# A fused attention, expert and MLP kernel: the order of the down products, the place of the small matmuls, and which engine takes the residuals

## The chip, the cores and the metric

The kernel runs on one core of a Trainium2 chip. The metric is the device time of one execution in microseconds (us), the median of three runs.

## The reference

Three layers follow each other, all in float32. Attention works in chunks of 64 positions; its result x (2304 tokens of 512) goes through a dense mixture of 8 experts, whose weights P come from eight rounds of Sinkhorn normalisation, and then through an MLP with a maximum of three products.

```python
attn = softmax(q_c @ k_c.T / 8)            # 4 x 8 heads, chunks of 64, head_dim 64
x = (attn @ v_c) -> (2304, 512)
logits = x @ w_gate; P = exp(logits - logits.max())
for _ in range(8):
    P /= P.sum(1, keepdims=True) + 1e-09
    P /= P.sum(0, keepdims=True) + 1e-09
    P *= N / E
out = sum over e of P[:, e:e+1] * (relu(x @ w1[e]) @ w2[e])     # F = 1024
h = max(out @ w1, out @ w2, out @ w3)                           # 768 wide
return h @ w_out
```

## The kernel before, in words

**Precision.** Every large product is made of three matmuls of a rounded type: high part by high part, high by low, low by high. So each operand exists twice: a copy in the rounded type (xh, wh, hh) and the residual that is left (xl, wl, hl). The helper `hilo` makes both: ScalarE copies, then GpSimd (or VectorE, where an engine is passed) subtracts.

**Items.** The 2304 tokens are split into three thirds of 768. The work is a list of items: 32 for each third of the expert layer (256 hidden units each, four to an expert), items 0 to 95, and then 9 for each third of the second MLP, items 96 to 122. In `up(n)` an item makes its hidden block by a seven-product scheme on 2 x 2 blocks: products P0 to P6, each of six matmuls with 384 columns, into three PSUM tiles: pa (P0, P2, P4, P6), pg (P1, P5) and pb (P3). The tiles keep accumulating, so between two products into one tile an evacuation must be done: ScalarE copies P0, P1 and P2 out as s0, s1 and s2 (L242), VectorE adds them to pb, pa and pg after P3, P4 and P5, as c0, c1 and c2 (L245). So P2 waits for s0, P4 for s2, P6 for c1, and the next item's P1 for c2. After P4 and P5 and P6, `finish` makes hh (ScalarE) and hl from c or from PSUM. In the expert items the 768-wide hl after P4 is GpSimd's (L216), after a relu in place by ScalarE (L215); the two of 384 are VectorE's (L219). In the MLP items the maximum with the earlier block is VectorE's (L227), and the last item of three (i = 2) calls `hilo` for hh and hl.

**Down products.** The hidden block of item n is used while item n + 1 runs. `down(n, q, j)` is one group: six matmuls of 512 columns into one PSUM bank, then an evacuation that adds it to the token block's accumulator, mostly on VectorE (L292, L288, L301). There are six groups an item (D1 to D6 below): first three that need hh and hl of the blocks 2 and 1, then three that need 0 and 3. The banks come from a pool of two (dn) up to item 24, and alternate between that and the other small pool (wk, two) from item 25 on. An expert item makes one group after each of P0 to P5. Of the MLP's items each of three makes two, after P2 and P4.

**What is put between.** `bg` is a table that says which functions are called at a position (item, product). At each position the order of issue is: the product and its evacuation; a transposed accumulator to be sent on (`y_out`), if one is due; preparation or fetch of weights; the functions of the table in the order in which they were entered; then the down groups. Engines run what they are given in that order. In the table stand: attention for token blocks 6 to 17 in items 1 to 13 (scores `att_qk` and `att_exp`, `att_norm` and `att_T`, `att_swap` with four DMAs, values `att_pv`, `x_save`, `gate`); the Sinkhorn steps in items 14 to 19, where `row_norm` (VectorE) is followed at the next spot by the TensorE sum `col_sum`; the decode of the second MLP's weights from 64-bit floats in items 33 to 94 (`decode_all`: 9 calls a job, in the last of which the DMA that stores dhi is issued and the next job's first VectorE step writes the same buffer); the next third's x (`x_put`, `x_cols`).

**DMAs** are all issued by SyncE, in order: raw weights, stores of the prepared weights in the first third, and from then on two fetches an item (`fetch` at P1, two items ahead, and `fetch2` at P2).

Of the kernel before, what the change touches and what calls it, by code (L numbers as in the profile page):

```python
# [47 lines left out]
def kernel(ctx: ExitStack, tc: tile.TileContext, qk, vv, wg, wts, wts2, out):  # L48
# [137 lines left out]
    mt = [None]  # L186

    def up(n):
# [21 lines left out]
        def finish(q, src):  # L210

            if not m2:
                nc.scalar.activation(out=hh[:, q], in_=src, func=AF.Relu)  # L213
                if q.start == 0:
                    nc.scalar.activation(out=src, in_=src, func=AF.Relu)  # L215
                    nc.gpsimd.tensor_tensor(out=hl[:, q], in0=src, in1=hh[:, q].bitcast(F32),  # L216
                                            op=ALU.subtract)
                    return
                nc.vector.scalar_tensor_tensor(out=hl[:, q], in0=src, scalar=0.0,  # L219
                                               in1=hh[:, q].bitcast(F32), op0=ALU.max, op1=ALU.subtract)  # L220
                return
            m = mt[0]
            if it["i"] == 0:
                if q.start == 3:
                    nc.scalar.copy(out=m[:, q], in_=src)
                return
            nc.vector.tensor_tensor(out=m[:, q], in0=src, in1=m[:, q], op=ALU.max)  # L227
            if it["i"] == 2:
                hilo(hh[:, q], hl[:, q], m[:, q])

        s = {}
        for pos, (wi, xi, b) in enumerate(PRODUCTS):
            ps = bank[b]
            for k in range(2):
                ws = slice(k * P, (k + 1) * P)
                for i, (x, y) in enumerate(((wh[n], vh), (wh[n], vl), (wl[n], vh))):
                    nc.tensor.matmul(ps, lhsT=x[:, wi, ws], rhs=y[:, xi, k], start=b not in begun,  # L237
                                     stop=k == 1 and i == 2, skip_group_check=True)
                    begun.add(b)
# [10 lines left out]
            else:  # L250
                finish(slice(3, 4), ps.unsqueeze(1))
            yield pos
# [94 lines left out]
    def x_put(pos):  # L347
        i = PRODUCTS[pos][1]
        hilo(xh[:, i], xl[:, i], xst[i], nc.vector if pos % 2 == 0 else None)
# [3 lines left out]
    def x_cols(j, r, eng, pl, xh, xl):  # L353
# [10 lines left out]
        nc.gpsimd.tensor_tensor(out=xl[:, 0:2, :, cols], in0=raw, in1=xh[:, 0:2, :, cols].bitcast(F32),  # L364
                                op=ALU.subtract)
        nc.gpsimd.tensor_tensor(out=xl[:, 2, :, cols], in0=r[:, 1, 2:4], in1=xh[:, 2, :, cols].bitcast(F32),
# [64 lines left out]
    def decode_all():  # L431
# [11 lines left out]
        for at_ in range(-2, len(jobs)):  # L443
# [13 lines left out]
            if i is not None:  # L457
                strassen_w([V[:, x] for x in range(4)], [V[:, 4 + x] for x in range(4)], nc.vector)
                yield
                hilo(hi, lo, V[:, 1:8])  # L460
                dst = lambda h: scr[p * 3 + i, h, :, :, k, :]
            else:
                hi, lo = (x[:, 0:4].rearrange("p i f -> p (i f)") for x in (hi, lo))
                hilo(hi, lo, V[:, 0:4].rearrange("p i f -> p (i f)"))
# [121 lines left out]
    def gate(t):  # L586
        p = wk.tile([P, E], F32, name="gp", tag="wk")
# [42 lines left out]
    for m in range(NT - NPE):  # L630
        t, n = NPE + m, 1 + m
        at(n, 0, lambda t=t: (att_qk(t), load_qk(t + 3), att_exp(t)))
        at(n, 2, lambda t=t: (att_norm(t), att_T(t)))
        at(n, 6, lambda t=t: att_swap(t))
        at(n + 1, 3, lambda t=t: (att_pv(t, wk), load_v(t + 3)))
        at(n + 1, 5, lambda t=t: x_save(t))
        at(n + 1, 6, lambda t=t: gate(t))
    for t in range(NPE):
        at(t // 2, 3 + 2 * (t % 2), lambda t=t: gate(t))
# [22 lines left out]
    for a in range(NPAIR + 1, first_of[3] - 1):  # L662
        for b in range(a % 2, 7, 2):
            at(a, b, lambda: next(dec, None))
# [4 lines left out]
    for k in range(1, 4):  # L669
# [6 lines left out]
        for pos in range(7):  # L676
            at(n0 - 1, pos, lambda pos=pos: x_put(pos))
# [12 lines left out]
    with tc.manual_schedule():  # L690
# [47 lines left out]
        for n in range(ni):  # L738
# [3 lines left out]
            quota = few = -(-len(pend) // ahead)  # L742
            for pos in up(n):
# [16 lines left out]
                if quota and pend and pos < 6 and (few > 2 or pos in (2, 4)):  # L760
                    down(*pend.pop(0))
                    quota -= 1
            if it["down"]:
                assert not pend
                pend = [(n, q, j) for q in (1, 0) for j in range(TS // 2)]
# [40 lines left out]
```

## Time and profile before

| | us |
|---|---|
| median of three runs | 1914.39 (1913.91 to 1915.68) |
| the profiled execution | 1914.13 |
| its span | 1912.3 |
| TensorE busy | 1869.4 (98%) |
| VectorE busy | 1126.6 (59%) |
| ScalarE busy | 689.2 (36%) |
| GpSimd busy | 638.2 (33%) |

The span is the time from the first to the last instruction of the profiled execution; the execution's own time has 1.8 us around it. Busy time of TensorE counts pipelined matmuls whose modelled ends overlap the next start, so the time between two starts says more than a duration. The profile names engines PE (TensorE), PEld (its weight loads), DVE (VectorE), ACT (ScalarE), POOL (GpSimd) and SP (SyncE); L269 is line 269 of the kernel.

### The profile page before, as it was taken

To read this page: it belongs to the slowest core of one execution; us is meant where nothing else is said; L and a number is where in the kernel's file an instruction comes from. 1 tells how busy PE (TensorE), PEld (TensorE's weight loads), DVE (VectorE), ACT (ScalarE), POOL (GpSimd) and SP (SyncE) were. 2 spreads that over 40 slices of the span, in tenths; PEclk is the share of its full clock that TensorE was granted. 3 is DMA by queue.
4 is the path that set the end of the run, shared out by engine and by line. 5 is a ranking of instruction groups with operands and counts; after the bars stand their busy time and mean duration, and the time that the engine had idled before them with its cause. 6 is when DMAs were issued, how large, how long until landed. Compare 5 with 4: busy or idle time off the path is not lost.

```text
span 1912.3 us, 26868 instructions
## 1 busy us (share of the span) xinstructions
PE 1869.4 (98%) x10397; PEld 1671.6 (87%) x10403; DVE 1126.6 (59%) x1768; ACT 689.2 (36%) x1204; POOL 638.2 (33%) x444
## 2 busy tenths in 40 slices
PE   6999999999999999999999999999999999999998
PEld 4988888888998888898889889888889888999997
DVE  7566564646784566565656655665566656545434
ACT  4554544454444232322322342222323233423221
POOL 5766666678882111111111122111211112212101
PEclk8999999999999999999999999999999999999999
DMA  7578867678888655556556665755656564757562
GB/s 249 195 280 290 305 255 274 263 281 299 320 326 312 229 202 222 212 212 234 203 212 236 220 236 190 265 203 211 215 203 249 201 237 165 268 217 277 208 252 95
DMA packets 167872, 455.30 MB, mean 238 GB/s; under 512 B 14272, under 2 KB 74688, under 8 KB 167744
## 3 DMA queue, kind: packets, MB, share of 16 engines
q1 hardware_dynamic: 167744, 453.58, 64.9%
q8 instruction: 82, 1.34, 0.3%
q14 instruction: 46, 0.38, 0.1%
HBM read 319.57 MB, written 132.38 MB: 236 GB/s over the span
## 4 chain that ended last, share of the span: by engine, by line
PE 89%; DMA 3%; DVE 3%; ACT 2%; POOL 1%; issue 1%; SPq 0%; ACTq 0%; DVEq 0%; POOLq 0%
PE dn L269 42%; PE pa L237 25%; PE pg L237 12%; PE pb L237 6%; DMA scr<-dhi 2%; PE gp L590 1%; PE s L499 1%; PE xp L578 1%; DMA w2l<-w2s 1%; PE warm L688 1%; DVE c L245 0%; DMA w2s<-w2l 0%; DVE acc L292 0%; ACT hh L213 0%; POOL wl L183 0%
## 5 line engine op out<-in xcount | busy, mean ns | idle before, releaser
L269 PE MATMUL dn<-w2h,hl 128*128 128x512 f32 x1260 | 501.1, 398 | 4.7 <-DVE hl L219 4.4
L269 PE MATMUL dn<-w2h,hh 128*128 128x512 f32 x1260 | 496.0, 394 | 5.7 <-ACT hh L213 3.5
L269 PE MATMUL dn<-w2l,hh 128*128 128x512 f32 x1260 | 498.0, 395 | 0.5 <-DMA w2l<-w2s 0.5
L292 DVE SCALAR_TENSOR_TENSOR acc<-dn,Pt,acc 128x512 f32<-128x512 f32 x438 | 327.3, 748 | 258.1 <-PE dn L269 255.2
L216 POOL TENSOR_TENSOR hl<-c,hh 128x768 fp32r<-128x768 f32 x96 | 177.9, 1854 | 842.6 <-ACT c L215 837.7
L237 PE MATMUL pa<-xh,wh 128*128 128x384 f32 x912 | 308.0, 338 | 7.1 <-ACT s L242 4.9
L237 PE MATMUL pa<-xl,wh 128*128 128x384 f32 x912 | 307.0, 337 | 0.0
L237 PE MATMUL pa<-xh,wl 128*128 128x384 f32 x912 | 305.5, 335 | 0.0
L213 ACT ACTIVATE hh<-c 128x768 fp32r<-128x768 f32 x192 | 131.7, 686 | 477.3 <-DVE c L245 476.8
L269 PEld LDWEIGHTS dn<-w2h,hl 128*128 128x128 f32 x1260 | 236.3, 188 | 58.5 <-DVE hl L219 7.8
L269 PEld LDWEIGHTS dn<-w2h,hh 128*128 128x128 f32 x1260 | 237.0, 188 | 38.7 <-ACT hh L213 5.3
L269 PEld LDWEIGHTS dn<-w2l,hh 128*128 128x128 f32 x1260 | 236.5, 188 | 30.5 <-DMA w2l<-w2s 1.2
L242 ACT COPY s<-pa 128x384 f32<-128x384 f32 x246 | 118.1, 480 | 256.7 <-PE pa L237 256.6
L237 PEld LDWEIGHTS pa<-xh,wh 128*128 128x128 f32 x912 | 171.5, 188 | 22.8 <-ACT s L242 6.8
L237 PEld LDWEIGHTS pa<-xl,wh 128*128 128x128 f32 x912 | 171.4, 188 | 13.3
L237 PEld LDWEIGHTS pa<-xh,wl 128*128 128x128 f32 x912 | 171.3, 188 | 0.0
L237 PE MATMUL pg<-xl,wh 128*128 128x384 f32 x456 | 153.8, 337 | 0.0
L237 PE MATMUL pg<-xh,wh 128*128 128x384 f32 x456 | 152.8, 335 | 0.4 <-DVE c L245 0.4
L237 PE MATMUL pg<-xh,wl 128*128 128x384 f32 x456 | 152.9, 335 | 0.0
L219 DVE SCALAR_TENSOR_TENSOR hl<-c,hh 128x384 fp32r<-128x384 f32 x96 | 111.6, 1162 | 61.7 <-ACT hh L213 61.1
L245 DVE TENSOR_TENSOR c<-pb,s 128x384 f32<-128x384 f32 x114 | 63.2, 554 | 92.3 <-PE pb L237 86.2
L242 ACT COPY s<-pg 128x384 f32<-128x384 f32 x123 | 59.1, 481 | 146.1 <-PE pg L237 145.8
(147 smaller groups left out, 2530.9 us busy)
## 6 DMA issues: line engine op xcount, KB each, us to landing
wh<-w1s SPq DMA_DIRECT2D x64, 896.0 KB, 4.6
wl<-w1s SPq DMA_DIRECT2D x64, 896.0 KB, 6.4
w2h<-w2s SPq DMA_DIRECT2D x64, 512.0 KB, 7.5
w2l<-w2s SPq DMA_DIRECT2D x64, 512.0 KB, 8.8
w1s<-wh SPq DMA_DIRECT2D x32, 896.0 KB, 7.4
w1s<-wl SPq DMA_DIRECT2D x32, 896.0 KB, 9.2
wh<-scr SPq DMA_DIRECT2D x27, 896.0 KB, 4.6
wl<-scr SPq DMA_DIRECT2D x27, 896.0 KB, 6.4
```

Source lines behind the costliest of these rows:

```text
L213: nc.scalar.activation(out=hh[:, q], in_=src, func=AF.Relu)
L216: nc.gpsimd.tensor_tensor(out=hl[:, q], in0=src, in1=hh[:, q].bitcast(F32), op=ALU.subtract)
L219: nc.vector.scalar_tensor_tensor(out=hl[:, q], in0=src, scalar=0.0, in1=hh[:, q].bitcast(F32), op0=ALU.max, op1=ALU.subtract)
L237: nc.tensor.matmul(ps, lhsT=x[:, wi, ws], rhs=y[:, xi, k], start=b not in begun, stop=k == 1 and i == 2, skip_group_check=True)
L242: nc.scalar.copy(out=s[pos], in_=ps)
L245: nc.vector.tensor_tensor(out=c[:, q], in0=ps, in1=s[other], op=ALU.add)
L269: nc.tensor.matmul(p, lhsT=h[:, hi, ts], rhs=w[:, f, :], start=(f == 0 and i == 0), stop=(f == 1 and i == 2))
L292: nc.vector.scalar_tensor_tensor(out=acc[t], in0=p, scalar=Pt[:, t, e:e + 1], in1=acc[t], op0=ALU.mult, op1=ALU.add)
L499: nc.tensor.matmul(ss[g][cs, hp, :], lhsT=a[r, hp, 0, cs], rhs=a[r, hp, 1, cs], start=True, stop=True)
L578: nc.tensor.matmul(p[64 * g:64 * g + 64, hp, :].rearrange("p (a q) -> p a q", a=2), lhsT=v[r, h * D:(h + 1) * D], rhs=aT[r, :, he, :], sta ...
L590: nc.tensor.matmul(p, lhsT=x[:, k, :], rhs=wgr[:, k, :], start=k == 0, stop=k == KD - 1)
L688: nc.tensor.matmul(p, lhsT=wones[:, 0:P], rhs=wones, start=True, stop=True)
```

## The change

Seven edits, all of order and place; the mathematics is the same.

- Down groups: expert items up to 24 make two each after P1, P3 and P5; from item 25 on three each after P2 and P5. The last item of all makes none while it runs: two groups of the item three before it are left and are run behind it, ahead of its own six.
- In the second and third third of the expert layer, the 768-wide hl is made like the others, by VectorE from c, without the relu in place.
- In the MLP's items hl is VectorE's, and issued one product later than hh (the list `later`).
- The residuals of the decode and of `x_cols` in the MLP move from GpSimd to VectorE; `x_put` swaps which of its seven residuals are VectorE's (three instead of four) and comes one position later.
- Attention in items 0 to 13: scores at position 6 of the item before (they were at 0), normalisation at 1 (2), swap at 4 (6), values at 6 of the same item (3 of the next) and in the pool dn (wk), `x_save` at 1 (5).
- Gates take PSUM from other pools; those of blocks 0 to 5 are called three at a time at position 6 of items 0 and 1 (one at a time, in items 0 to 2).
- The decode is not called in items 63 and 64.

```diff
@@ up(n), finish
-                if q.start == 0:
+                if q.start == 0 and it["sb"] == 0:
                     nc.scalar.activation(out=src, in_=src, func=AF.Relu)
                     nc.gpsimd.tensor_tensor(out=hl[:, q], in0=src, in1=hh[:, q].bitcast(F32),
                                             op=ALU.subtract)
...
             if it["i"] == 2:
-                hilo(hh[:, q], hl[:, q], m[:, q])
+                nc.scalar.copy(out=hh[:, q], in_=m[:, q])
+                later.append(lambda: nc.vector.tensor_tensor(
+                    out=hl[:, q], in0=m[:, q], in1=hh[:, q].bitcast(F32), op=ALU.subtract))
...
+            rest = later[:]
+            later.clear()
...
+            for f in rest:
+                f()
             yield pos
@@ x_put
-        hilo(xh[:, i], xl[:, i], xst[i], nc.vector if pos % 2 == 0 else None)
+        hilo(xh[:, i], xl[:, i], xst[i], nc.vector if pos % 2 else None)
@@ x_cols
+        rest = nc.gpsimd if pl is ap_ else nc.vector
-        nc.gpsimd.tensor_tensor(out=xl[:, 0:2, :, cols], in0=raw, in1=xh[:, 0:2, :, cols].bitcast(F32),
+        rest.tensor_tensor(out=xl[:, 0:2, :, cols], in0=raw, in1=xh[:, 0:2, :, cols].bitcast(F32),
...
@@ decode_all
-                hilo(hi, lo, V[:, 1:8])
+                hilo(hi, lo, V[:, 1:8], nc.vector)
...
@@ the table
-        at(n, 0, lambda t=t: (att_qk(t), load_qk(t + 3), att_exp(t)))
-        at(n, 2, lambda t=t: (att_norm(t), att_T(t)))
-        at(n, 6, lambda t=t: att_swap(t))
-        at(n + 1, 3, lambda t=t: (att_pv(t, wk), load_v(t + 3)))
-        at(n + 1, 5, lambda t=t: x_save(t))
-        at(n + 1, 6, lambda t=t: gate(t))
+        at(n - 1, 6, lambda t=t: (att_qk(t), load_qk(t + 3), att_exp(t)))
+        at(n, 1, lambda t=t: (att_norm(t), att_T(t)))
+        at(n, 4, lambda t=t: att_swap(t))
+    for m in range(NT - NPE):
+        t, n = NPE + m, 1 + m
+        at(n, 6, lambda t=t: (att_pv(t, dn), load_v(t + 3)))
+        at(n + 1, 1, lambda t=t: x_save(t))
+        at(n + 1, 6, lambda t=t: gate(t, ps_b))
     for t in range(NPE):
-        at(t // 2, 3 + 2 * (t % 2), lambda t=t: gate(t))
+        at(t // 3, 6, lambda t=t: gate(t, ps_b if t % 3 == 0 else ps_g if t % 3 == 1 else dn))
...
-            at(a, b, lambda: next(dec, None))
+            if a not in (first_of[2] - 1, first_of[2]):
+                at(a, b, lambda: next(dec, None))
...
-            at(n0 - 1, pos, lambda pos=pos: x_put(pos))
+            a = 7 * (n0 - 1) + min(pos + 1, 6 if k == 3 else 7)
+            at(a // 7, a % 7, lambda pos=pos: x_put(pos))
@@ the main loop
-            quota = few = -(-len(pend) // ahead)
+            few = -(-len(pend) // ahead)
+            quota = few if n < ni - 1 else 0
...
-                if quota and pend and pos < 6 and (few > 2 or pos in (2, 4)):
-                    down(*pend.pop(0))
-                    quota -= 1
+                if few > 2:
+                    run = (2 if pos in (1, 3, 5) else 0) if n <= NT + 6 else 3 if pos in (2, 5) else 0
+                else:
+                    run = 1 if pos in (2, 4) else 0
+                for _ in range(run):
+                    if quota and pend:
+                        down(*pend.pop(0))
+                        quota -= 1
             if it["down"]:
-                assert not pend
-                pend = [(n, q, j) for q in (1, 0) for j in range(TS // 2)]
+                assert len(pend) == (2 if n == ni - 1 else 0)
+                pend += [(n, q, j) for q in (1, 0) for j in range(TS // 2)]
+        for f in later:
+            f()
         for d in pend:
             down(*d)
```

## Rows read from the trace of the kernel before

**Rows 1.** The page, part 1: busy us of each engine, its share, instructions.

```profile
PE 1869.4 (98%) x10397; PEld 1671.6 (87%) x10403; DVE 1126.6 (59%) x1768; ACT 689.2 (36%) x1204; POOL 638.2 (33%) x444
```

**Rows 2.** The waits of TensorE: who it waited for, total us, times, longest.

```profile
PE pa L237 <- ACT s L242: 7.3, 9, 1.4
PE dn L269 <- DVE hl L219: 4.4, 4, 1.2
...
PE dn L269 <- ACT hh L213: 3.5, 2, 2.5
PE pa L237 <- DVE c L245: 2.2, 4, 0.7
PE dn L269 <- ACT hh L182: 2.0, 1, 2.0
...
PE yp L310 <- DVE acc L292: 1.2, 1, 1.2
PE cp L616 <- DVE cs L612: 1.0, 1, 1.0
```

**Rows 3.** Timeline of TensorE, item 52: start, duration, engine, line, operation, out<-in.

```profile
902.03 0.40 PE L269 MATMUL dn<-w2h,hl 128*128 128x512 f32 x1
902.26 0.33 PE L237 MATMUL pa<-xh,wh 128*128 128x384 f32 x1
...
903.14 0.34 PE L237 MATMUL pa<-xh,wl 128*128 128x384 f32 x1
903.31 0.39 PE L269 MATMUL dn<-w2h,hh 128*128 128x512 f32 x1
```

**Rows 4.** Timeline of TensorE around a gate (item 7) and scores (item 12).

```profile
189.13 0.95 PE L590 MATMUL gp<-wgr,xr 128*128 128x8 f32 x8
189.94 0.42 PE L237 MATMUL pa<-xh,wh 128*128 128x384 f32 x1
...
266.14 0.34 PE L237 MATMUL pa<-xh,wl 128*128 128x384 f32 x1
266.41 0.97 PE L499 MATMUL s<-qk 64*64 64x64 f32 x32
267.31 0.50 PE L269 MATMUL dn<-w2h,hh 128*128 128x512 f32 x1
267.65 0.40 PE L269 MATMUL dn<-w2l,hh 128*128 128x512 f32 x1
267.89 0.39 PE L269 MATMUL dn<-w2h,hl 128*128 128x512 f32 x1
```

**Rows 5.** Timeline of VectorE: a Sinkhorn row step, and part of another.

```profile
330.39 0.29 DVE L608 TENSOR_REDUCE rs<-Pt 128x18 f32<-128x144 f32 x1
...
331.57 0.44 DVE L612 TENSOR_REDUCE cs<-Pt 128x8 f32<-128x144 f32 x1
...
340.85 1.62 DVE L609 TENSOR_SCALAR rs<-rs 128x18 f32<-128x18 f32 x1
```

**Rows 6.** Timeline of SyncE and VectorE in item 36: first fetch, decode step, evacuation.

```profile
654.79 0.32 SPq L171 DMA_DIRECT2D wh<-w1s  x1
...
667.20 0.43 DVE L409 TENSOR_SCALAR scm<-w 128x512 int32<-128x512 int32 x1 [6.61 <-DMA scr<-dhi]
667.54 0.74 DVE L292 SCALAR_TENSOR_TENSOR acc<-dn,Pt,acc 128x512 f32<-128x512 f32 x1
```

**Rows 7.** Timeline of VectorE in item 101 of the MLP: its three maxima.

```profile
1675.60 0.96 DVE L227 TENSOR_TENSOR m<-c,m 128x768 f32<-128x768 f32 x1
...
1678.04 1.73 DVE L227 TENSOR_TENSOR m<-c,m 128x384 f32<-128x384 f32 x1
1679.69 0.54 DVE L227 TENSOR_TENSOR m<-pa,m 128x384 f32<-128x384 f32 x1
```

**Rows 8.** The attention swap: SyncE's issue of its DMAs, and all landings by tile eT.

```profile
172.03 2.41 SPq L549 DMA_DIRECT2D aT<-eT  x4
...
DMA to landing us min/median/max: 1.8/1.9/5.3
```

More of the change, by code (lines that the diff above doesn't have):

```diff
@@ L186 @@
     mt = [None]
+    later = []
     def up(n):
@@ L363, in x_cols @@
         nc.scalar.copy(out=xh[:, 2, :, cols], in_=r[:, 1, 2:4])
-        nc.gpsimd.tensor_tensor(out=xl[:, 0:2, :, cols], in0=raw, in1=xh[:, 0:2, :, cols].bitcast(F32),
+        rest = nc.gpsimd if pl is ap_ else nc.vector
+        rest.tensor_tensor(out=xl[:, 0:2, :, cols], in0=raw, in1=xh[:, 0:2, :, cols].bitcast(F32),
                                 op=ALU.subtract)
-        nc.gpsimd.tensor_tensor(out=xl[:, 2, :, cols], in0=r[:, 1, 2:4], in1=xh[:, 2, :, cols].bitcast(F32),
+        rest.tensor_tensor(out=xl[:, 2, :, cols], in0=r[:, 1, 2:4], in1=xh[:, 2, :, cols].bitcast(F32),
                                 op=ALU.subtract)
@@ L463, in decode_all @@
                 hi, lo = (x[:, 0:4].rearrange("p i f -> p (i f)") for x in (hi, lo))
-                hilo(hi, lo, V[:, 0:4].rearrange("p i f -> p (i f)"))
+                hilo(hi, lo, V[:, 0:4].rearrange("p i f -> p (i f)"), nc.vector)
                 dst = lambda h: scro[p, h, :, k]
@@ L583, in x_save, with gate @@
         nc.sync.dma_start(out=xs[t], in_=raw_of(t))
-    def gate(t):
-        p = wk.tile([P, E], F32, name="gp", tag="wk")
+    def gate(t, pp):
+        p = pp.tile([P, E], F32, name="gp", tag=pp.name)
         x = raw_of(t)
```

## The prediction

> **What bounds the kernel now.** I read the page's busy line first, then TensorE's own waits, then the timeline of TensorE at the three places where its order changes, and last the two engines that feed it.
>
> TensorE is busy for 98% of the span, the next engine, VectorE, for 59% [rows 1]. So only two things can pay: fewer TensorE nanoseconds for the same matmuls, or fewer of its waits. The second purse is small. The waits that the change can reach add up to 7.3 + 4.4 + 3.5 + 2.2 + 2.0 + 1.2 + 1.0 = 21.6 us [rows 2], 1.1% of the span. A wait costs a little more than its row says: the first matmul after another kind of work goes out 0.34 us before the next one, where 0.24 is usual [rows 4]. So I add 0.1 us per restart.
>
> Is there a purse in the order itself? A down matmul is followed by the next after 0.24 us [rows 4] and by an up matmul after 0.23; an up matmul by a down after 0.17, and by an up after (903.14 - 902.26) / 5 = 0.18 [rows 3]. A change between the two kinds costs nothing, so runs of two or three groups give nothing by being runs. They only move the cover: which other work lies between a product and the one that waits for its evacuation. From the same rows a product (six matmuls) is 1.05 us and a down group 1.4 us.
>
> **1. Runs of two and three.** Before, positions 0 to 5 of an expert item each end with a group. After, items 25 on run P0 P1 P2 DDD P3 P4 P5 DDD P6.
>
> *What it removes.* The first group of an item now starts two products (2.1 us) later. The two waits on hh at the starts of the second and third third (3.5 us, longest 2.5) shrink to at most 0.4, and the wait of the first transposed output (1.2) goes, since outputs are now sent two products after a finished run: with five restarts 5.2 us less. The one wait on w2l (a row below those shown, 0.5) goes too: 0.6. Where the second MLP begins stands the longest of the nine waits on s (1.4) and, by a row below those shown, one of 0.4 on VectorE's add; both come from x casts and residuals late on their engines. Two x casts still stand before s0, which keeps 0.5 with its restart: minus 1.5. Some small waits beside groups: 0.4. Sum: **minus 7.7**.
>
> *What it doesn't remove.* The eight waits of 4.4 and 2.2 us are four events of one kind. VectorE's first decode step waits 6.61 us for the DMA that empties the tile it reuses [rows 6]; everything behind it on VectorE is late. That item began at 654.79, with the weights' fetch ahead of the slow DMA; the step runs 12.4 us into the item, whatever VectorE does, since the bytes queue behind the fetch. In the new order the step is issued after P2 and before the evacuations of D1, D2, D3. There are four banks, so D5 needs D1's: ideal 3.1 + 4.2 + 3.1 + 1.4 = 11.8 us into the item, available at 12.4 + 0.43 + 0.74 = 13.6: a 1.8 us wait. VectorE then has two more evacuations, three adds and a residual to do, so the next item's P1 waits some 0.7 (its bank) and P2 some 0.8 (s0 behind hh on ScalarE); with three restarts 3.5 us, between 1.8 (the first wait alone) and 4.5. Counting the steps of the decode through the items, with two items now left out, this falls behind P2 in items 36, 56 and 78: 10.5 us. The fourth event, in item 61, falls behind P3 with c0 already done and P6 2 us away: nothing. The two calls left over run together at the end of item 94, where a cast that waits for VectorE stands before s0: 0.9. Before, the four events cost 6.6 us in those rows and three or four restarts and a short first wait each, some 0.8 an event: 9.8. So **plus 1.6**, between minus 9 and plus 5.
>
> *What it adds: the Sinkhorn steps.* They keep their positions, but positions are no longer 2.4 us apart. Eight times a row step on VectorE is followed, one position later, by a TensorE sum that waits for it. Three of these pairs (positions 4 to 5 twice, 2 to 3 once) now have only one product, 1.05 us, between them. The row step takes 331.57 + 0.44 - 330.39 = 1.62 us on a quiet VectorE, and it starts some 0.8 us after the product (the add before it): 1.4 us of wait, twice. The third meets GpSimd's weight residuals, where one step of the five alone takes 1.62 us instead of 0.17 [rows 5]: 1.8. Behind the waiting sum stand the next down groups. With restarts 4.9, less the 1.0 of before and its restart: **plus 3.8** (1.5 to 6).
>
> **2. Small attention matmuls side by side.** Before, a scores block costs 0.10 on entry (0.27 instead of 0.17 after the last up matmul), 0.90 for the 32 matmuls and the way out, and 0.10 of restart; the value products are alike, and a gate is 0.81 plus 0.1 [rows 4]. After, the three follow each other at position 6, in the order scores(t+1), gate(t-1), values(t), by the order in which they are entered in the table. The gate stands between the other two. So changes from full to 64-row matmuls stay four an item, and only two of three restarts go: 0.2 x 12 = 2.4, and 0.4 from six early gates now in two blocks: **minus 2.8**.
> The Trainium skill, "TensorEngine Tiling (Array Packing)", Key Properties, says that changing the tiling mode, not just the tile, drains TensorE. By that rule this order saves no drain, which is the sum taken; had scores and values touched, an entry and an exit of about 0.2 us more would go per item, 2.6 us in all. The entry of 0.27 us against 0.17 agrees with the rule.
>
> *New waits.* The values now fill the two dn banks that the next item's first run needs. ScalarE frees them after the exp, which waits for VectorE's scores work; I reach 5.0 us after P6 for both the bank and D1: 0.1 us, at eleven items **plus 1.1** (0 to 6). In item 1 the third gate waits in the same way, 1.5 **once**. The swap of attention halves moves from position 6 to 4 and its reader from three positions into the next item to this item's 6. Four DMAs take SyncE 2.41 us to issue and land 1.9 us after [rows 8]. After P4 come an add, hh, relu and the copy, some 3.2 us, against 4.9 from P4 to the end of P6; so the first DMA is issued 1.7 us before that end and the last lands about 1.9 us after it. Scores and gate fill 1.9 us, and the second half of the values, which needs the last DMA, starts at 2.3. That is nothing as a rule. Three items also send six finished accumulators, ahead of it in the queue; I take 0.3 us each: **plus 1** (0 to 38, if all twelve landed at the 5.3 us of the slowest row).
>
> **3. GpSimd out of the last blocks.** Nothing of GpSimd is on TensorE's path but by delay of VectorE: a max that is 0.54 us elsewhere took 1.73 beside a GpSimd residual [rows 7]. Then hh, then s0 on ScalarE, then P2, which waits (7.3 - 1.4) / 8 = 0.74 us, eight times [rows 2]. After, the max is short, but the 768-wide residual (0.96, the duration of the 768-wide max) stands on VectorE before the last max. So the last max comes only 0.2 us earlier, and 0.2 x 8 = **minus 1.5** of the 7.3 goes (0 to minus 6, if it fitted in a gap).
> In the expert thirds two and three VectorE gains 0.96 an item and loses contention; ScalarE loses one relu. Both have room: P6 waits for the second add only, three groups later.
>
> **4. The end.** Before, the last six groups wait 2.0 us for hh [rows 2] and, by a row below those shown, 0.3 for the residual, with a restart each and a short start: 2.7. After, two groups are held back and run there, 2.8 us of cover for about 2.9 of chain, which leaves 0.1: **minus 2.6**.
>
> Gate banks, the residuals of x on VectorE, x casts one position later: nothing; VectorE has over 40% idle to hide them [rows 1], and where an x cast falls before s0 at a third's start it has 0.2 us to spare.
>
> **Sum.** -7.7 + 1.6 + 3.8 - 2.8 + 1.1 + 1.5 + 1.0 - 1.5 - 2.6 = -5.6. The profiled execution took 1914.13, its span 1912.3, with 1.8 around it that the change leaves alone; it lies 0.26 below the median of the three runs, which I carry over: 1914.39 - 5.6 = **1908.8**.
>
> **Rivals.**
> *The decode blocks vanish.* For it: runs of three leave TensorE longer without need of VectorE than single groups did. Against: the bank of D1. If the DMA lands 2 us sooner, the 10.5 us go: 1898.
>
> *The swap lands late.* It decides on whether the last of its four DMAs lands more than 2.3 us after P6. For it: the slowest row is 5.3, and expert weights, stores and accumulators share that queue. Against: the median of 1.9. Were it 1.3 us late on average in twelve items with a restart each: +17, 1925. It decides from 0.5 us an item on, where 12 x 0.5 eats the forecast's 5.6; from 0.8 on the kernel is measurably slower.
>
> *Nothing on balance.* Sinkhorn at its upper bound, the D1 waits at 0.3 and no gain in the waits on s: +2 +2 +1.5, 1914. For it: three quarters of my gain is waits of which only the start is moved.
>
> *The change does not do what it says*: the gate between scores and values is in the forecast already.
>
> **Chances.** Forecast 0.45, decode vanishing 0.2, nothing on balance 0.2, late swap 0.15. A measurement of this kernel tells about 0.2%, 3.8 us, from no change: faster is below 1910.6. The forecast lies there in about three of four cases: 0.34 + 0.2 + 0.04 = 0.58 faster; 0.27 same; 0.15 slower. The range takes in most of the vanishing case and the bounds of the Sinkhorn and bank terms: 1898 to 1918.
>
> **What would show it.** TensorE's waits: on hh L213 (now under 0.5 us), on the dn bank or acc in items 36, 56, 78 (about 1.8 each), on cs three times of 1.4 to 1.8, on s still about eight; values' matmuls starting within 0.3 us of the gate; the last group without a wait over 0.3. Wrong it is if attention items take much over 18.7 us, if decode items show no wait, or if a down group after an up matmul is not 0.17 us behind it.

## The result, and the profile after

The changed kernel takes **1926.35 us** (median of 14 runs, 1917.92 to 1929.83); beside it the kernel before took 1914.96 (14 runs, 1912.03 to 1917.81). The ratio is 1.0053, 95% interval 1.0043 to 1.0062: slower, by more than the 0.2% that can be told. Forecast were 1908.8 and a range that ends at 1918. The profiled execution took 1926.37, 12.2 more than before.

The page, part 1, and the row of granted clock from part 2 (40 slices of 48 us, tenths of full speed) of the changed kernel:

```profile
PE 1880.3 (98%) x10397; PEld 1693.5 (88%) x10403; DVE 1153.4 (60%) x1892; ACT 627.0 (33%) x1140; POOL 424.0 (22%) x320
...
PEclk7899999999899999999999999999999999999999
```

GpSimd fell from 638 to 424 us as meant [rows 1]. But TensorE, with the same 10397 matmuls, is busy for 11 us more: the matmuls themselves got slower. Its waits from 47 us on (who, total, times, longest):

```profile
PE dn L276 <- DVE acc L299: 10.9, 5, 3.1
PE pa L242 <- ACT s L247: 8.7, 13, 3.3
PE cp L624 <- DVE cs L620: 3.2, 3, 1.2
PE xp L586 <- DMA aT<-eT: 3.1, 5, 1.0
PE dn L276 <- ACT s L247: 0.3, 1, 0.3
```

The waits of [rows 2] on hh, hl, c and the transposed outputs are gone, as forecast. Those on s and cs have grown, and new ones stand on aT (the swapped attention halves that the values read) and behind the evacuations (acc): 26.2 us in all where the seven rows had 21.6. That is not yet 12. The rest is the clock. Busy time in windows of the changed kernel (window, length, busy us of PE, PEld, DVE, ACT, POOL, then granted clock, DMA share, GB/s):

```profile
57.30:64.10 6.80, 6.80 (x25) 6.66 (x26) 4.59 (x11) 2.59 (x8) 4.02 (x5) 0.50 0.96 367
81.20:88.00 6.80, 6.80 (x27) 6.80 (x28) 2.06 (x5) 1.71 (x6) 0.30 (x1) 0.50 1.00 386
238.20:241.60 3.40, 3.40 (x13) 3.40 (x12) 2.31 (x5) 1.59 (x4) 0.00 (x0) 0.51 0.96 351
296.30:299.70 3.40, 3.40 (x12) 3.21 (x11) 0.00 (x0) 1.88 (x4) 1.30 (x1) 0.50 0.98 335
501.10:507.90 6.80, 6.01 (x17) 5.43 (x18) 2.70 (x5) 0.00 (x0) 2.44 (x2) 0.50 0.71 259
514.70:518.10 3.40, 3.14 (x8) 2.56 (x9) 1.04 (x3) 0.00 (x0) 1.51 (x3) 0.50 1.02 398
692.20:695.60 3.40, 3.40 (x9) 2.65 (x9) 2.49 (x5) 0.84 (x1) 0.00 (x0) 0.50 0.08 29
1613.80:1620.60 6.80, 5.46 (x14) 4.73 (x15) 2.48 (x4) 4.05 (x7) 2.88 (x2) 0.50 0.73 243
```

In eight stretches, 40.8 us together, the granted clock is 0.5, the lower of TensorE's two levels (1.2 instead of 2.4 GHz). Before, it is never below 1.0 between 46 and 1912 us; the row of the page before:

```profile
PEclk8999999999999999999999999999999999999999
```

At half clock one up matmul follows another after 0.32 instead of 0.18 us (the two at 59.78 below) and one down matmul another after 0.43 instead of 0.23 (item 25, below), so up to half of the 40.8, some 20 us, is lost in them. What comes ahead of each differs. At the end of item 0 (57.3) there is no wait at all, only small matmuls:

```profile
54.76 0.98 PE L507 MATMUL s<-qk 64*64 64x64 f32 x32
55.67 3.79 PE L598 MATMUL gp<-wgr,xr 128*128 128x8 f32 x24
...
59.78 0.52 PE L242 MATMUL pa<-xl,wh 128*128 128x384 f32 x1
60.10 0.52 PE L242 MATMUL pa<-xh,wl 128*128 128x384 f32 x1
```

Three gates that take 0.95 each alone [rows 4] take 3.79 in a row, and the clock is down. In item 1, and at 238 and 296, small matmuls with a wait for a DMA among them come first; in item 1:

```profile
77.33 0.98 PE L507 MATMUL s<-qk 64*64 64x64 f32 x32
78.15 0.68 PE L586 MATMUL xp<-aT,v 64*64 64x64 f32 x16
79.42 0.68 PE L586 MATMUL xp<-aT,v 64*64 64x64 f32 x16 [0.58 <-DMA aT<-eT]
80.03 4.23 PE L598 MATMUL gp<-wgr,xr 128*128 128x8 f32 x24
```

In item 25 long waits come first; TensorE, and VectorE, whose evacuation of the first down group stands behind two folds of stored sums (L331):

```profile
501.89 0.80 PE L276 MATMUL dn<-w2h,hh 128*128 128x512 f32 x1 [3.11 <-DVE acc L299]
502.48 0.63 PE L276 MATMUL dn<-w2l,hh 128*128 128x512 f32 x1
502.91 0.63 PE L276 MATMUL dn<-w2h,hl 128*128 128x512 f32 x1
...
514.96 0.79 PE L276 MATMUL dn<-w2h,hh 128*128 128x512 f32 x1 [2.79 <-DVE acc L299]
```

```profile
496.45 4.72 DVE L331 SCALAR_TENSOR_TENSOR acc<-u,Pt,acc 128x512 f32<-128x512 f32 x2
501.10 1.40 DVE L299 SCALAR_TENSOR_TENSOR acc<-dn,Pt,acc 128x512 f32<-128x512 f32 x2
```

Why a third group waits for the first there can be read in the code. The runs of three begin while item 25 is current, but `down` alternates between the pools when the block it uses is later than 24, and in item 25 that block is 24. The first two runs of three have two banks, not four. (The description of the kernel before has the alternation "from item 25 on"; that holds for the block that is used, and block 25 is used while item 26 runs.)

Where the 12.2 us came from, by items (an item lasts from its first up matmul to the next item's), after minus before, beside the terms of the forecast:

| part | forecast | measured |
|---|---|---|
| attention, gates: items 0 to 13 | -2.8 + 1.1 + 1.5 + 1.0 = +0.8 | **+12.1** |
| Sinkhorn: items 14 to 18 | +3.8 | +2.4 |
| item 25 | nothing of its own | **+10.6** |
| decode: items 36, 37, 56, 57, 61, 62, 76 to 79 | +0.7 | -0.6 |
| decode's last two calls: item 95 | +0.9 | **+6.1** |
| runs, all other expert items and 96 | -7.7 | -12.9 |
| MLP's waits: items 97 to 121 | -1.5 | -2.4 |
| end: item 122 | -2.6 | -2.9 |

These sum to 12.4; item 0 starts 0.2 earlier. Five rows came out as forecast or better; three cost 27 us more than forecast.

### The profile page after: what moved, and what is told of

Same layout as the page of the kernel before. It is cut to its first block, busy times and chain, and to the rows that moved or that the text cites. A ratio compares the mean times of both kernels' runs of the same rounds, so it can differ in the third digit from the quotient of the medians.

```text
span 1924.5 us, 26677 instructions
## 1 busy us (share of the span) xinstructions
PE 1880.3 (98%) x10397; PEld 1693.5 (88%) x10403; DVE 1153.4 (60%) x1892; ACT 627.0 (33%) x1140; POOL 424.0 (22%) x320
## 4 chain that ended last, share of the span: by engine, by line
PE 89%; DVE 4%; DMA 2%; ACT 2%; issue 1%; POOL 0%; SPq 0%; DVEq 0%; ACTq 0%
PE dn L276 42%; PE pa L242 25%; PE pg L242 11%; PE pb L242 7%; DVE c L250 1%; DMA scr<-dhi 1%; DVE m L228 1%; PE gp L598 1%; ACT hh L214 1%; DMA aT<-eT 1%; PE warm L700 1%; PE s L507 1%; PE xp L586 1%; DVE acc L299 1%; DMA scr<-dlo 0%
## 5 line engine op out<-in xcount | busy, mean ns | idle before, releaser
L299 DVE SCALAR_TENSOR_TENSOR acc<-dn,Pt,acc 128x512 f32<-128x512 f32 x438 | 313.2, 746 | 169.7 <-PE dn L276 169.6
L242 PE MATMUL pa<-xh,wh 128*128 128x384 f32 x912 | 312.2, 342 | 7.4 <-ACT s L247 7.4
L183 POOL TENSOR_TENSOR xl<-xf,xh 128x768 fp32r<-128x768 f32 x12 | 23.6, 1971 | 1008.6 <-ACT xh L182 1006.0
L220 DVE SCALAR_TENSOR_TENSOR hl<-c,hh 128x384 fp32r<-128x384 f32 (+1 forms) x160 | 149.2, 933 | 137.1 <-ACT hh L214 137.1
L214 ACT ACTIVATE hh<-pa 128x384 fp32r<-128x384 f32 x96 | 47.1, 491 | 180.1 <-PE pa L242 180.1
```

The lines of the kernel that those rows point to most:

```text
L183: (eng or nc.gpsimd).tensor_tensor(out=l, in0=v, in1=h.bitcast(F32), op=ALU.subtract)
L299: nc.vector.scalar_tensor_tensor(out=acc[t], in0=p, scalar=Pt[:, t, e:e + 1], in1=acc[t], op0=ALU.mult, op1=ALU.add)
```

## The experiments

The theory: the waits went as worked out but for item 25 and the end of the decode, and what was priced at 0.1 us per restart is dear where TensorE stood or did only small matmuls for a while, because the clock halves behind it. The rivals: the attention halves that land late, alone; a clock that falls for reasons of its own; runs that cost time whatever their banks.

**e1: four banks in item 25.**

```diff
-        turn[0] ^= n > NT + 6
+        turn[0] ^= n > NT + 5
```

> The alternation between the two pairs of banks starts one item sooner, at item 25, where the runs of three start. Theory (item 25 is long because the third group of each run of three had only two banks, waited 3.1 and 2.8 us for an evacuation, and the clock halved after it): item 25 falls from 26.2 to about 15.7 us, no granted clock below 1.0 in it, and the whole from 1926.4 to about 1916. Rival (the first runs of three cost this whatever banks they have, or the clock drops belong to this stretch): item 25 stays above 20 us and the whole within 3 us of the changed kernel.

Measured: 1916.28 us, ratio to before 1.0005 (0.9991 to 1.0019). Item 25 takes 15.57 us, at full clock. So what item 25 lost is the banks'.

**e2: the waits of item 25, filled with matmuls.**

```diff
+        if n == NT + 6 and j == 2:
+            fill = wk.tile([P, DM], F32, name="fill", tag="wk")
+            for _ in range(13):
+                nc.tensor.matmul(fill, lhsT=hh[:, HIDX[0, q], 0:P], rhs=w2h[n][:, 0, :], start=True, stop=True)
```

> Changed kernel with 13 more matmuls (128x512, into a bank that nothing reads) between the second and the third group of both runs of item 25: some 3.1 us of TensorE work each, in the place of waits of 3.11 and 2.79 us. Theory (the clock falls because TensorE stood idle): the third group waits under 0.5 us, the granted clock stays at 1.0, and item 25 takes 15.6 + 2 x 3.1 = about 21.8 us instead of 26.2, shorter with more work in it. Rival (the clock falls for another reason at that place and the waits alone cost 5.9): item 25 takes 26 us or more, with the clock at 0.5 in it as before.

Item 25 took 21.64 us (the whole 1919.22, in one execution). The timeline of TensorE and the two halves of the item:

```profile
498.62 2.88 PE L274 MATMUL fill<-w2h,hh 128*128 128x512 f32 x12
501.34 0.39 PE L280 MATMUL dn<-w2h,hh 128*128 128x512 f32 x1
```

```profile
492.50:503.00 10.50, 10.50 (x52) 9.25 (x52) 7.44 (x10) 4.55 (x8) 10.42 (x8) 1.00 0.86 347
503.00:514.10 11.10, 11.10 (x55) 9.61 (x54) 8.00 (x10) 2.11 (x3) 5.59 (x6) 1.00 0.85 291
```

The third group starts 8.8 us into the item, nearly as late as in the changed kernel (9.2), but TensorE was kept busy; the clock column stays at 1.00, and the item is 4.6 us shorter than the 26.21 of the changed kernel with 26 more matmuls in it. Not all of that is the fill. e3 and e10 below leave item 25 as it is, and there it took 21.84 and 21.92 us: a wait of 0.58 in item 24 comes first (e2 has it too), the two waits of item 25 are then 0.7 and 3.59, and one stretch at half clock follows. The second wait in e3, at half clock from 511.5 on:

```profile
511.80 0.79 PE L276 MATMUL dn<-w2h,hh 128*128 128x512 f32 x1 [3.59 <-DVE acc L299]
```

What holds is that the clock fell in item 25 in all three kernels that wait there and not in the one that fills the waits, and that 6 us of added matmuls made the item no longer. By the changed kernel's own trace 5.9 of its 10.6 us are waits; the other 4.7 go with the 10.2 us at half clock. Nor does half clock follow every long wait: item 95, untouched, waited 3.33 us in this run without it, and took 19.2 instead of 21.7.

**e3: the last decode calls earlier.**

```diff
+    for a in (90, 92):
+        at(a, 5, lambda: next(dec, None))
     at(first_of[3] - 2, 6, lambda: [None for _ in dec])
```

> The two decode calls left over at the end of item 94 are made in items 90 and 92, so that only the stores are left for item 94. Theory: the wait of 3.3 us on s in item 95 and the half clock after it go, item 95 falls from 21.7 to about 15.7 us, items 90 to 93 gain no wait over 0.5 us; the profiled run is some 6 us shorter in that stretch. Rival (item 95 is late for the x casts of the next third, not for the decode calls): item 95 keeps a wait over 2 us and takes over 19 us.

Item 95 took 15.57 us, with no wait (the whole 1916.93, in one execution); items 90 to 93 stayed at 15.57 too. The profile of the changed kernel shows the chain that this removes: the two calls, issued at the end of item 94, stand on VectorE behind three evacuations, and ScalarE's copy of V stands before s0. VectorE, then ScalarE:

```profile
1610.20 2.06 DVE L299 SCALAR_TENSOR_TENSOR acc<-dn,Pt,acc 128x512 f32<-128x512 f32 x3
...
1613.36 0.69 DVE L461 TENSOR_TENSOR V<-V,scm 128x512 f32<-128x512 f32 x1
```

```profile
1614.09 0.62 ACT L182 CAST dhi<-V 128x512 fp32r<-128x512 f32 x1 [3.84 <-DVE V L461]
1614.61 0.47 ACT L247 COPY s<-pa 128x384 f32<-128x384 f32 x1
```

**e4: both mends, and the old attention order** (the table and banks of before; `gate(t, wk)`).

> Both of these mended, and the attention blocks and gates put back to the positions and banks that they had before the change; runs, Sinkhorn steps and casts as in the changed kernel. Theory (items 0 to 13 lose 12.1 us by the regrouped attention alone, items 25 and 95 lose 10.6 and 6.1 by their waits): 1926.4 - 12.1 - 10.6 - 6.1 = about 1898 us, faster than before the change by 0.8%; clock above 0.99 after 60 us. Rival (runs of two in the attention items cost the time, or clock drops come elsewhere instead): items 0 to 13 stay 5 us or more above before, the whole at 1905 or more.

Measured: 1897.17 us, ratio 0.9912 (0.9895 to 0.9928). Items 0 to 13 stand 0.8 us below before, and the clock is at 1.0 from 45 us to the end. The three places account for the loss: runs and GpSimd's part together are gains.

**b1: the attention part alone on the kernel before** (the diff's edits to `gate` and the attention table, nothing else).

> The kernel before the change with the attention and gate part of the change alone: single down groups, GpSimd's work and everything else as before. Theory (that part alone costs what items 0 to 13 lost, whatever the down groups do, through long blocks of small matmuls and half clock behind them): 8 to 12 us more than before, 1922 to 1926, half clock after the three early gates at the ends of items 0 and 1. Rival (the part is a gain of 1 to 3 us and loses only together with the runs of two, whose evacuations hold the banks of the values): within 4 us of before.

Measured: 1930.69 us, ratio 1.0087 (1.0072 to 1.0102), more than the theory had. Items 0 to 13 take 17.9 us more. Its waits from 45 to 340 us and its clock over items 0 to 13:

```profile
PE xp L578 <- DMA aT<-eT: 3.4, 5, 1.0
PE pa L237 <- ACT s L242: 0.6, 1, 0.6
```

```profile
46.00:318.00 272.00, 267.91 (x1968) 240.29 (x1967) 132.51 (x234) 130.57 (x242) 163.14 (x126) 0.94 0.70 254
```

Waits of 4.0 us explain less than a quarter of it. The clock of 0.94 over the 272 us comes from six stretches at half clock, 30.6 us in all, in which up to 15 us are lost.

**e5, e6, e7: what in the attention order does it.** All three have both mends. e5 puts the six early gates back one by one; e6 also makes the swap a position sooner; e7 also moves the later gates out from between scores and values.

```diff
-        at(t // 3, 6, lambda t=t: gate(t, ps_b if t % 3 == 0 else ps_g if t % 3 == 1 else dn))
+        at(t // 2, 3 + 2 * (t % 2), lambda t=t: gate(t, wk))       # e5, e6, e7
-        at(n, 4, lambda t=t: att_swap(t))
+        at(n, 3, lambda t=t: att_swap(t))                          # e6, e7
-        at(n + 1, 6, lambda t=t: gate(t, ps_b))
+        at(n + 1, 4, lambda t=t: gate(t, wk))                      # e7
```

> Changed kernel with the banks of item 25 and the two decode calls mended, and the six early gates one by one in the first three items as before the change, instead of three in a row at the ends of items 0 and 1. The rest of the attention order is the changed one. Theory (the clock halves after a long stretch of small matmuls, whether or not a wait stands in it: scores and three gates are 4.7 us of them): no half clock at the ends of items 0 and 1, these two items fall from 37.2 to about 28.2 us together, the whole to 1926.4 - 16.7 - 9 = about 1901. Rival (the loss in items 0 and 1 is the new position of the scores or the first aT): items 0 and 1 stay over 33 us.

> As the last, and the swap of the attention halves one position sooner (3 instead of 4), so that its DMAs are issued one product and, in half of the items, a down run earlier. Theory (aT lands late by 0.4 to 1.0 us in five items of the changed kernel, and each such wait stretches the block of small matmuls): the waits on aT go, fewer or no half clock in items 2 to 13, 2 to 6 us less than the last kernel, about 1897. Rival (aT is late for the queue, whose order is the same): waits on aT of 0.4 us and more stay in three or more items, the time stays within 2 us.

> As the last, and the gate of the token block before moved from position 6 to position 4, in a work bank, so that scores and values alone stand side by side: 2.0 us of small matmuls instead of 3.0. Theory (the length of the block of small matmuls decides): no granted clock below 1.0 from 60 us to the end, undisturbed attention items about 0.1 us longer than 18.64; the whole 1896 to 1899, at or under the last. Rival (what decides is that scores and values touch at all, or the wait in front of the values): half clock in two or more items of 2 to 13, over 1900.

e5: 1904.99 us, ratio 0.9952 (0.9935 to 0.9969), 4 more than expected; items 0 and 1 took 29.7 us together (expected 28.2) and were at full clock, but in items 3 and 4 half clock still followed a wait on aT (1.00) and another of 0.30, and once more the decode's wait in item 78 (1.74). e6: 1896.41, ratio 0.9905 (0.9890 to 0.9919), as expected: no wait on aT, and full clock from 45 us on, though three kinds of small matmuls still stand in a row. The swap's DMAs landed later after their issue than in the changed kernel (3.9 us at the median instead of 1.9); the gain is the earlier issue. One such row, and the clock of items 0 to 13:

```profile
149.03 0.98 PE L507 MATMUL s<-qk 64*64 64x64 f32 x32
149.93 1.06 PE L598 MATMUL gp<-wgr,xr 128*128 128x8 f32 x8
150.92 0.98 PE L586 MATMUL xp<-aT,v 64*64 64x64 f32 x32
```

```profile
46.00:300.00 254.00, 254.00 (x1982) 229.24 (x1981) 144.25 (x235) 127.78 (x245) 165.33 (x128) 1.00 0.75 277
```

e7: 1894.02, ratio 0.9893 (0.9879 to 0.9908), 2 us below the expectation, which had the sign of its first term wrong: an undisturbed item takes 18.38 to 18.45 us instead of 18.64, not 0.1 more. Here scores and values touch, and a change between 64-row and full matmuls goes. The forecast had put that at 0.2 us an item, for an order that the change did not choose. The Trainium skill, "TensorEngine Tiling (Array Packing)", Key Properties, says that a change of tiling mode drains TensorE; these 0.2 us agree.

**e10: fill between the early gates.** Six full matmuls ahead of each gate of the first six blocks, in the changed kernel.

```diff
...
+            for i in range(6):
+                nc.tensor.matmul(full[:, 64:64 + W], lhsT=wh[t // 3][:, 0, 0:P], rhs=xh[:, 0, 0], start=True, stop=True)
```

> Changed kernel with six full matmuls (128x384, read by nobody) ahead of each of the six early gates, some 1.05 us each time, 6.3 us more of work in items 0 and 1. Theory (the clock halves there because scores and three gates of 8 columns follow each other): granted clock 1.0 from 50 to 90 us, items 0 and 1 together 29.7 + 6.3 = 36.0 us, not longer than the 37.2 without the extra work. Rival (the clock falls there for another reason): half clock at about 57 and 81 us again, items 0 and 1 over 42 us.

Windows over the end of item 0, most of item 1, and its end:

```profile
56.10:62.90 6.80, 6.80 (x75) 6.73 (x75) 5.08 (x10) 1.95 (x6) 4.95 (x5) 1.00 0.64 205
62.90:79.00 16.10, 16.10 (x88) 14.31 (x89) 4.29 (x6) 10.29 (x19) 9.29 (x6) 1.00 0.50 195
79.00:87.30 8.30, 7.71 (x106) 7.54 (x102) 4.53 (x10) 1.85 (x6) 2.41 (x4) 1.00 0.83 260
```

The clock stays at 1.00, as the theory had it, even past the wait of 0.59 on aT. The time expected was worked out wrongly: items 0 and 1 took 39.1 us, not 36.0, because the 29.7 of e5 hold only four of the six gates (two more are 1.9) and a filled gap costs up to 1.17, not 1.05: 29.7 + 1.9 + 7.0 = 38.6. Against the changed kernel's 37.2 that is 7.0 us of added work for 1.9 of time, 5.1 us given back. The whole gained nothing by it: 1931.48 us in its one execution, since items 2 to 13, which the edit leaves alone, lost 8 us against before (the changed kernel 3), mostly behind waits on aT.

**b2: GpSimd's part alone on the kernel before.**

> The kernel before the change with the GpSimd part alone: residuals on VectorE and behind the next max, x casts one position later; attention, gates, down groups and decode positions as before. Theory (it shortens the last MLP items by 0.3 us each and little else): 2 to 4 us less than before, about 1911. Rival (most of what the changed kernel gains in the thirds two and three, 5.3 us at the start of the second MLP and 2.6 each in the pairs of items 61 and 76, comes from this part and not from the runs): 8 us less or more, 1906 or under.

Measured: 1910.37 us, ratio 0.9973 (0.9964 to 0.9983). The MLP's items give 2.3 and item 122 gives 1.0; item 64, where the last third of the expert layer begins (the expectation calls it the start of the second MLP), gives 2.1 of the 5.3 that the whole change has there, item 96, where the second MLP does begin, 1.1 of 1.8, and items 61 and 76 nearly nothing. So the rest is the runs' or, at item 64, that of the decode calls left out there, which no run takes apart. In the items behind the decode's late steps four waits on hh stand where before had four on hl (4.4 us, [rows 2]), with half clock behind two of them:

```profile
PE dn L276 <- ACT hh L214: 6.8, 4, 1.9
```

**e8: the waits that the forecast had named, taken out**, on e4's order: decode steps behind the first run's evacuations, each Sinkhorn sum behind a down run, the MLP's 768-wide residual behind the last max, runs of three and four banks from item 23.

```diff
-        turn[0] ^= n > NT + 6
+        turn[0] ^= n > NT + 3
...
-        for b in range(a % 2, 7, 2):
+        for b in ((0, 3, 4, 6), (1, 3, 5))[a % 2]:
...
-    spots = [(n + a, b) for a in range(6) for b in range(1, 6)]
+    spots = [(n, 1), (n, 2)] + [(n + 1 + a, b) for a in range(4) for b in (1, 2, 3, 3, 4, 5)]
...
-            rest = later[:]
-            later.clear()
+            rest = []
+            if not m2 or pos != 5:
+                rest = later[:]
+                later.clear()
...
-                    run = (2 if pos in (1, 3, 5) else 0) if n <= NT + 6 else 3 if pos in (2, 5) else 0
+                    run = (2 if pos in (1, 3, 5) else 0) if n <= NT + 4 else 3 if pos in (2, 5) else 0
```

> Both mends, the attention order of before the change, and the named waits taken out: decode steps of even items at positions 0, 3, 4, 6 instead of 0, 2, 4, 6, so that the late step is issued behind the evacuations of the first run; each Sinkhorn sum with a down run between its row step and itself; the hidden residual of the last MLP block's position 4 behind the last max; runs of three from item 23 on, with four banks. Theory (the waits of items 36, 56 and 78 come from the evacuations queued behind the late decode step, those on cs from the short cover, those of 0.45 us from the residual ahead of the max): these items fall by about 3.0 us each, the Sinkhorn waits by 3.2, the last MLP items by 0.45 eight times, item 24 by 0.8; 1897.2 less some 15 to 17 us: about 1881. Rival (the late DMA moves its wait somewhere else): the gain is under 8 us, with waits of over 1 us on VectorE's acc or add left in decode items.

**e9: e8 with the attention order of e7.**

> The kernel without the named waits, with the attention order of the run in which scores and values stand together, the gate at position 4, the swap at position 3 and the early gates one by one. Theory (both gains are in different items and add): items 0 to 13 fall by the 3.5 us by which that order stood below the old one in its profile, from 1881.5 to about 1878. Rival (runs, Sinkhorn steps or the earlier decode positions collide with it): 1881 or more.

e8 took 1881.53 us, ratio 0.9831 (0.9813 to 0.9849), as expected; e9 **1874.18**, ratio 0.9795 (0.9779 to 0.9812), 4 below its expectation. In the profiles 3.1 of the 8.4 us between e8 and e9 lie in items 0 to 13, as expected, and 4.6 ahead of item 0, in the start-up that both share, where the clock is not steady in any run; so how much of the 7.4 between the medians is the order is not settled. e9 is faster than both kernels. All of TensorE's waits in e8 from 48 us on:

```profile
PE pa L244 <- ACT s L249: 1.9, 5, 0.5
PE pa L244 <- DVE c L252: 0.2, 1, 0.2
PE gp L600 <- ACT xr L590: 0.2, 1, 0.2
```

## Why the prediction was wrong, step by step

Three places of the sum failed and cost 27 us more than forecast: the small matmuls side by side (+0.8 forecast, +12.1 measured), the banks in item 25 (nothing, +10.6) and the decode's last two calls (0.9, 6.1). In all three a part of the loss is half clock, for which the sum had no term: it priced every wait and every row of small matmuls as at full clock. The rest is waits that it did not see or took too small. The other rows came out as forecast or better.

**1. Runs.** The gain was -12.9 where -7.7 was forecast. Of it 0.07 us lie in each of 46 undisturbed items, which the forecast had at nothing, and 3.2 us in items 64 and 96 come with GpSimd's part alone, as b2 shows. But the same step took it for granted that four banks serve every run of three. In item 25 they don't, by one item's offset between two conditions in the code: +10.6, a size and a place that stand in no term. e1 shows it. The forecast named the banks (D5 needs D1's) and did not ask from which block on they alternate.

The decode step did as forecast: the late step waits for its DMA, the evacuations stand behind it, and D5 waits for D1's bank, 1.90, 1.48 and 1.65 us in items 36, 56 and 78 (1.8 forecast), the next s0 0.5 (0.8); the 0.7 of the next P1 did not come (the forecast's 3.5 an event adds up to 3.6 by its own terms). Half clock behind such a wait need not cost: items 36 and 37 took 34.89 us together with it in the changed kernel and 34.36 to 34.69 without in e1, e2 and e4 to e7. VectorE in item 36 (compare [rows 6]):

```profile
690.84 0.43 DVE L417 TENSOR_SCALAR scm<-w 128x512 int32<-128x512 int32 x1 [8.96 <-DMA scr<-dlo]
691.18 2.06 DVE L299 SCALAR_TENSOR_TENSOR acc<-dn,Pt,acc 128x512 f32<-128x512 f32 x3
```

e8 moves the step behind those evacuations, and items 36, 56 and 78 take 15.57 us. The two calls at the end of item 94, 0.9 in the forecast, cost 6.1: a wait of 3.3, since the forecast left out the three evacuations ahead of the calls on VectorE, and half clock behind it. e3 shows it.

**Sinkhorn** was right in mechanism: three waits of 1.19, 0.81 and 1.19 (1.4, 1.8 and 1.4 forecast), +2.4 instead of +3.8; the step beside GpSimd's residual was over-priced. In e8, with a down run in between, they are gone.

**2. Small matmuls side by side** is the step that failed. It was priced at -2.8 by counting entries and exits. That gain exists, but smaller: e6's undisturbed items take 18.64 against 18.76 in the old order, 0.12 each, where 0.2 was taken. The terms beside it, a bank wait of 1.1 and the third gate's 1.5, never appeared: no wait stands there. What stands there is the clock, for which the sum had no term at all. Before, a scores block, a value block and a gate stood apart, each about 1 us, and the clock never fell. After, five kernels of this study have the three gates behind the scores at the ends of items 0 and 1, and in all five the clock was at half behind both. In items 2 to 13 of all runs, the 54 undisturbed rows of scores, gate and values (2.73 us from full matmul to full matmul) had no half clock behind them; of the 33 rows stretched (seven of them gate and values alone), mostly by waits on aT, 20 had. Nor does the clock fall for reasons of its own: with neither three gates in a row nor a late aT it stood at 1.0 from 48 us to the end in e4 and e6 to e9, and fell in b2 only behind two long waits.

The swap was right in place and too small: five waits on aT of 0.4 to 1.0, 3.1 us, where +1.0 was taken. Its DMAs landed in 1.9 us at the median [rows 8], but in items 8 and 9, two of the five, in 2.3 to 3.9:

```profile
DMA to landing us min/median/max: 1.8/1.9/3.9
```

The rival "the swap lands late" came nearest to the time (1925), and its mechanism is about half of the loss in items 0 to 13. The changed kernel takes 14.8 us more there than e6: 7.7 in items 0 to 2, with the early gates, and 7.0 in items 3 to 13, with four of the five waits on aT (2.5 us) and half clock behind two of them. e5 to e6, the swap alone, is 8.6 us between medians. But the rival had waits alone, 1.3 us in each of twelve items, and neither the gates nor the clock nor item 25; that the time fits is luck.

**3. GpSimd** was right in mechanism. The last max of an MLP item stands behind the 768-wide residual, as forecast, and s0 still comes 0.45 to 0.49 us late eight times. VectorE in item 101 (compare [rows 7]):

```profile
1695.66 0.56 DVE L228 TENSOR_TENSOR m<-c,m 128x384 f32<-128x384 f32 x1
1696.14 0.95 DVE L231 TENSOR_TENSOR hl<-m,hh 128x768 fp32r<-128x768 f32 x1
1697.01 0.55 DVE L228 TENSOR_TENSOR m<-pa,m 128x384 f32<-128x384 f32 x1
```

Seven of the eight items with that wait gained 0.30 to 0.38 instead of 0.2; item 99 lost 0.18. e8 puts the residual behind the max, and the wait is gone.

**4. The end** gave 2.9 instead of 2.6.

**The restart.** Throughout, a wait was priced as its row plus 0.1 us, from rows in which the clock stood at 1.0. That is right for most waits here. It is wrong for some of the long ones: after 320 us, of the 29 gaps of 1.5 to 2.1 us between full matmuls in all traces 6 had half clock behind them, and of the 13 longer ones 8, for 3.4 or 6.8 us. The Trainium skill, "TensorE: Matmul & The Clock Gate", section "A second HAM failure mode: psum-queue depth-cycling", says that short idle times between groups of matmuls, as the banks go round, can make the clock swing between its levels. In item 25, where TensorE waits for a bank to come round, the clock does fall, behind waits of 3.11 and 2.79 us; a swing from many short idle times no run here shows.

What stays open: why of two waits alike one is followed by half clock and another not (item 36: 1.90 us with it in the changed kernel, 2.07 without in e4). The 14 runs of the changed kernel spread over 12 us, the 4 of e9 over 4, which would fit; it was not tested. So the split of a loss by items is that of one execution: item 25 lost 10.6 us in the changed kernel and 6.2 and 6.3 in e3 and e10.

## What to carry to other kernels

Look at the granted clock before pricing a new order on TensorE: here it fell behind long waits, but also behind long rows of small matmuls that the profile counts as busy. The three early gates were better apart; with full matmuls in between the clock held too, but the added work cost more than it gave back. Rows of 2.7 us kept the clock as long as no wait stood in them. When a rule changes at a certain item (banks, runs), find for each condition which item's number it tests: one off made one of the dearest items of this kernel. A chain that waits for a DMA is cheap when nothing of the critical path is queued behind it on its engine.

## What was not expected of the hardware

More work took no more time: with 26 further matmuls in the place of its waits item 25 took 21.64 us, against 26.21, 21.84 and 21.92 in the three kernels that wait there; the clock stayed at its upper level with them and fell in each of the three. And a gate of eight matmuls with 8 columns takes 0.95 to 1.06 us at full clock alone or between others, but three in a row behind the scores took 3.79 and 4.23 us, with the clock at half from the middle of the first such row on.
